# Work moved between VectorE, GpSimd and ScalarE where the attention heads give way to the sequence product

## The chip, the cores and the metric

One core of one Trainium2 chip runs the whole program. The metric is device time in microseconds of one execution; the time of the kernel before is the median of three runs. The engines are TensorE (PE in the profile, its weight loads PEld), VectorE (DVE), ScalarE (ACT), GpSimd (POOL) and SyncE (SP), which issues all the transfers that matter here. Each engine executes its own instructions in program order and waits for the others at semaphores.

## The reference

The network has four layers on one sequence of 2048 rows and 640 columns: attention, Fourier mixing, attention, Fourier mixing. Each adds its result to its input, and each normalizes its input first.

```python
def _A_ref(x, wqkv, wo):
    B, S, D = x.shape
    H = 32; Dh = D // H; W = 256
    qkv = (x @ wqkv).reshape(B, S, 3, H, Dh).transpose(2, 0, 3, 1, 4)
    q, k, v = qkv[0], qkv[1], qkv[2]
    scores = jnp.einsum("bhqd,bhkd->bhqk", q, k) * (Dh ** -0.5)
    scores = jnp.where(mask, scores, -1e9)  # 0 <= row - column < 256
    o = jnp.einsum("bhqk,bhkd->bhqd", _softmax(scores), v)
    return o.transpose(0, 2, 1, 3).reshape(B, S, D) @ wo

def _B_ref(x, dft_seq_re, dft_seq_im, dft_hid_re, dft_hid_im):
    a = jnp.einsum("bsd,ed->bse", x, dft_hid_re)
    b = jnp.einsum("bsd,ed->bse", x, dft_hid_im)
    return jnp.einsum("ts,bse->bte", dft_seq_re, a) - jnp.einsum("ts,bse->bte", dft_seq_im, b)

x = x + _A_ref(_layernorm(x), A_wqkv, A_wo)
x = x + _B_ref(_layernorm(x), ...)      # and both once more
```

## The kernel before

**Precision.** All large products are taken three times in a reduced float format: each operand is cut into a high half (ScalarE, L157) and a low half, the rest (a subtraction at L163, on VectorE or on the engine that the caller names). Product = high·high + high·low + low·high.

**The passage from heads to sequence product** is what the change touches; it occurs twice, once after each attention layer. At the end of the heads the output projection is done in two parts. The first three of its five input chunks are done while the heads still run (*partials*, L847); the last two ("late" chunks, k = 3 and 4) come afterwards, one 128-row tile t = 0 to 15 at a time (*late*, L925 to L964). The late operands are loaded per block of four tiles, one *late set* sb = 0 to 3 (*load_o*, L738): two chunks arrive by DMA (L751) with the reciprocal softmax sums (L757), are multiplied (L769, tile names cr, x, pt) and cut into halves in the tiles kp (L157, L163). These steps are not done at once but posted: *post(delay, fn)* puts fn into a slot, and *tick* runs what is due, so a posted instruction enters its engine's program order some slots later. After the heads a tick is counted for every 0.65 us of TensorE work (*spend*).

**A tile of late** is two products of 6 matmuls (L170) in the banks 5 and 6 alternately, each followed by an addition on VectorE (L940, or L934 for the first four tiles) that frees the bank. Then follow the statistics (L215, L217, L219, L946), the inverse root as a power on GpSimd (L948), two ScalarE steps that normalize (L904, L901), and the cuts of the normalized rows x (*split_x*, tile name big). Tiles 0 to 7 give the upper half of x, tiles 8 to 15 the lower; for the lower half the sum of two tiles is made (*sum1*, L1008) and a difference (*sum3*, L1012). The last two tiles take a shorter way, with VectorE normalizing their last 256 columns (*norm_last*, L916).

**The sequence product** multiplies the transposed DFT matrix, loaded in tiles of 128 x 1024 (L1103, DRAM tensor c), with x. Symmetries of the matrix and a seven-product scheme reduce the matmuls: for a (sb, part) of the output the order is a list of units (phase, j), and for the first (sb, part) it is: a1 for j = 0 to 7, a2 for j = 0 to 6, b7 0, a2 7, b7 1, b5 0, b5 1, b 2 to 7, g 0 to 7. a1 units need tile j of x, a2 units need tile j + 8, so these units are run between the tiles of late (*after_heads*, L972). The other three (sb, part) have phases a, b, g only.

A unit is run by *seq(n)* (L1191): it issues loads for a few units ahead, cuts the matrix of unit n + 1 (*cut_to*), prepares x for n + 1 (*x_to*), issues the matmuls (L1220) and cuts the matrix of unit n + 2. Cutting an a1 matrix first makes a difference t1 of its two halves (L1138), used later in a2; a b matrix has a difference on VectorE (L1146); a g matrix has two (L1149 t1, L1150 p) and three cuts. The b7 units have their difference at L1111 and two cuts. The sums of x for phase b are made pair by pair on VectorE (*sum4_to*, L1020 and L1021).

All eight PSUM banks are in use at the end of phase b. After the last unit of a phase *gather* (L1248) copies the sums out of the banks: for a1 three copies on ScalarE (L1269, L1270), for a2 one on ScalarE and one on VectorE (L1272, L1273), for b an addition, two ScalarE copies and two VectorE copies (L1264, L1280, L1283), which free banks for the first g unit. Its stores are kept in a list and issued one unit later or more.

What sets the order is the program text with its posted slots; there is no planner. The lines on which the steps rest:

```python
 768        eng, at = (nc.vector, (6, 8)) if self.after else (nc.gpsimd, (8, 10))
 948            self.post(2, lambda st=st: nc.gpsimd.tensor_tensor(
1138                nc.gpsimd.tensor_tensor(out=t1, in0=q, in1=p, op=OP.subtract)
1149                nc.gpsimd.tensor_tensor(out=t1, in0=p, in1=t1, op=OP.subtract)
1156                self.split(c[0], c[1], x, eng=nc.gpsimd if ph == "a2" and j > 5 else None)
1239        self.cut_to(n + 2)
1240        if last:
1241            self.gather(sb, part, ph)
```

Of the kernel before, what the change touches and what calls it, by code (L numbers as in the profile page):

```python
# [33 lines left out]
EARLY = 3  # L34
# [3 lines left out]
FIRST = 7  # L38
LATE = 9
PACE = 0.65  # L40


CHUNKS = ((0, 16, 0, 8), (0, 16, 8, 16), (16, 24, 0, 16), (24, 32, 0, 16), (0, 32, 16, 20))
# [18 lines left out]
class Net:  # L62
# [222 lines left out]
    def attention(self, xsrc, xdst):  # L285
        self.take_small(F32)
        for name in ("kp", "qp"):
            for i in (1, 0):
                if (name, i) != ("kp", 0):
                    self.take_qk(name, i)  # L290
        self.after, self.wide, self.lead = False, False, True
        self.late_o, self.late_t = [], 0
        self.before_heads(xsrc)
        self.heads(xsrc, xdst, self.fourier_hook)
        self.after_heads()
# [442 lines left out]
    def load_o(self, o, sb, k, raw=None, rr=None):  # L738

        nc = self.nc  # L740
        raw = self.raw()[:, :512] if raw is None else raw
        h0, h1, d0, d1 = CHUNKS[k]
        for q in range(h0 // 4, h1 // 4):
            while (q, sb) not in self.stored:
                if self.heavy:
                    self.relieve()
                self.tick()
        cols = slice(sb * 512, (sb + 1) * 512)
        nh, nd = h1 - h0, d1 - d0
        src = self.od[h0:h1, 1 + d0:1 + d1, cols]  # L750
        nc.sync.dma_start(raw, src if nh >= nd else src.rearrange("h d s -> d h s"))  # L751
        if k and CHUNKS[k - 1][:2] == (h0, h1):
            rr = self.turn.pop(("rr", sb))
        else:
            rr = self.next("rr") if rr is None else rr
            src = self.rd[sb, h0:h1, :]
            nc.sync.dma_start(rr, src.unsqueeze(1).broadcast_to([nh, nd, 512]) if nh >= nd else  # L757
                              src.unsqueeze(0).broadcast_to([nd, nh, 512]))
            self.turn["rr", sb] = rr
        o["left"] = o.get("left", 0) + 1  # L760

        def done():
            o["left"] -= 1

        def cut():
            self.split(o[k][0], o[k][1], raw, eng=nc.gpsimd)
            self.post(0 if k < EARLY else 3, done)
        eng, at = (nc.vector, (6, 8)) if self.after else (nc.gpsimd, (8, 10))
        self.post(at[0], lambda: eng.tensor_tensor(out=raw, in0=raw, in1=rr, op=OP.mult))  # L769
        self.post(at[1], cut)  # L770

    def complete(self, o):
        while o["left"]:
# [121 lines left out]
    def late(self, xsrc, xdst, hook):  # L895
# [29 lines left out]
        for t in range(NB):  # L925
# [9 lines left out]
            else:  # L935
# [8 lines left out]
            st = self.stats(xw, False)  # L944
            nm = self.ln.tile([P, 2], F32, name="nb", tag="nb")
            nc.vector.tensor_scalar_mul(nm[:, 0:1], st[0][:, 0:1], -1.0)  # L946
            fast = t >= NB - 2
            self.post(2, lambda st=st: nc.gpsimd.tensor_tensor(  # L948
                out=st[1][:, 1:2], in0=st[1][:, 0:1], in1=self.half, op=OP.pow))
            if NB // 2 - 1 <= t < NB - 1:  # L950
                self.post(4, lambda t=t: self.sum3(t - NB // 2 + 1))
            if fast:
# [19 lines left out]
    def after_heads(self):  # L972
# [4 lines left out]
        while True:  # L977
            t = self.late_t
            self.poll_late(99)
            while t < NB and not self.ready_late():  # L980
                if not self.unit():
                    self.tick()
                self.poll_late(99)
# [11 lines left out]
                self.tick()  # L995
        for _ in range(20):
            self.tick()
        assert not self.posted
        self.slot = None


# [118 lines left out]
    def cut_to(self, n):  # L1120
        nc = self.nc
        while self.n_cut <= min(n, len(self.order) - 1):
# [4 lines left out]
            ph, j = self.order[u][2:]  # L1127
            if ph == "b7":
                if j:
                    self.staged(u, 0, nc.gpsimd)  # L1130
                    self.staged(u, 1)
                    self.staged(u, 2)
                continue
            t1, r = self.t1[j], self.raw_of.pop(u, None)
            if r is not None:
                p, q = r[:, :512], r[:, 512:]
            if ph in ("a", "a1"):
                nc.gpsimd.tensor_tensor(out=t1, in0=q, in1=p, op=OP.subtract)  # L1138
                src = [p] + ([t1] if ph == "a" else [])
            elif ph == "a2":  # L1140
                src = [t1]
# [3 lines left out]
            elif ph == "b":  # L1145
                nc.vector.tensor_tensor(out=p, in0=q, in1=p, op=OP.subtract)  # L1146
                src = [q, p]
            else:
                nc.gpsimd.tensor_tensor(out=t1, in0=p, in1=t1, op=OP.subtract)  # L1149
                nc.vector.tensor_tensor(out=p, in0=t1, in1=q, op=OP.subtract)  # L1150
                src = [q, t1, p]
            out = []
            for x in src:
                c = self.ring.popleft()
                self.ring.append(c)
                self.split(c[0], c[1], x, eng=nc.gpsimd if ph == "a2" and j > 5 else None)
                out.append(c)
            self.cut_of[u] = out

    def x_to(self, n):  # L1160
# [30 lines left out]
    def seq(self, n):  # L1191
# [42 lines left out]
        if ph == "g":  # L1234
            mul("m1", x[0], 0, 256, c[0])
            mul("c1", x[0], 256, 128, c[0])
            mul("m6", x[1], 0, 256, c[1])
            mul("m4", x[0], 384, 256, c[2])
        self.cut_to(n + 2)
        if last:  # L1240
            self.gather(sb, part, ph)

    def leave(self, n=9):
# [4 lines left out]
    def gather(self, sb, part, ph):  # L1248
# [16 lines left out]

        mid = self.pt[2][:, 1024:]
        if ph in ("a", "a1"):
            for i in range(2):
                nc.scalar.activation(m1[i], banks("m1")[i], AF.Copy)  # L1269
            nc.scalar.activation(mid, banks("c1")[0], AF.Copy)  # L1270
        if ph in ("a", "a2"):
            nc.scalar.activation(m5[0], banks("m5")[0], AF.Copy)  # L1272
            nc.vector.tensor_copy(m5[1], banks("m5")[1])  # L1273
        if ph == "b":
            out = self.raw()[:, :512]
            add(nc.vector, out, banks("c2")[0], mid)
# [250 lines left out]
```

## Time and profile before

| | |
|---|---|
| median of 3 runs | 2259.83 us (2257.31 to 2260.46) |
| profiled execution, its own time | 2260.54 us |
| its span, first to last instruction | 2258.8 us |
| mean granted TensorE clock | 0.987 |
| first passage, late tiles and first (sb, part) up to g 0 | about 549 to 672 us of the span |
| second passage | about 1665 to 1788 us of the span |

A row of the view by stretches gives start and end in us from the span's start, the length, the busy time (and number of instructions) of TensorE, weight loads, VectorE, ScalarE and GpSimd, the granted clock as a fraction of full speed, the share of the DMA engines and GB/s. A row of the waits names who waited for whom: us in total, how often, the longest. A row of the groups gives line, engine, operation, tiles out<-in, shapes and count, then busy us and mean ns of one, then the idle time of the engine before it and what ended it. A row of the timeline has start, duration, engine, line and tiles, and in brackets the idle time before it with the engine that ended it. A row of the chain of work that ended last has start, duration and who held it.

### The profile page before, as it was taken

To read this page: it belongs to the slowest core of one execution; us is meant where nothing else is said; L and a number is where in the kernel's file an instruction comes from. 1 tells how busy PE (TensorE), PEld (TensorE's weight loads), DVE (VectorE), ACT (ScalarE), POOL (GpSimd) and SP (SyncE) were. 2 spreads that over 40 slices of the span, in tenths; PEclk is the share of its full clock that TensorE was granted. 3 is DMA by queue.
4 is the path that set the end of the run, shared out by engine and by line. 5 is a ranking of instruction groups with operands and counts; after the bars stand their busy time and mean duration, and the time that the engine had idled before them with its cause. 6 is when DMAs were issued, how large, how long until landed. Compare 5 with 4: busy or idle time off the path is not lost. (4 is left out here: it accounts for less than half of the span.)

```text
span 2258.8 us, 49233 instructions
## 1 busy us (share of the span) xinstructions
PE 2169.5 (96%) x18064; PEld 1817.8 (80%) x18064; DVE 1489.8 (66%) x3705; ACT 1114.2 (49%) x2401; POOL 1014.9 (45%) x1540
## 2 busy tenths in 40 slices
PE   7999999998889999999999999999998899999999
PEld 7987777677768888889999777777776688888999
DVE  6347788674787868772461578876746968678522
ACT  2117777656454545541331277776655545446310
POOL 3037776767745223230130477678676433232200
PEclk9999999899999999999999999998999999999999
DMA  5545656775435353655446465668753354545553
GB/s 180 179 143 186 195 185 198 220 208 163 138 117 182 125 183 131 214 170 168 161 165 190 142 194 179 202 195 233 198 170 120 117 183 139 168 156 201 164 166 100
DMA packets 217297, 385.57 MB, mean 171 GB/s; under 512 B 38880, under 2 KB 85472, under 8 KB 217056
## 3 DMA queue, kind: packets, MB, share of 16 engines
q1 hardware_dynamic: 217056, 382.43, 53.2%
q8 instruction: 143, 2.34, 0.5%
q14 instruction: 98, 0.80, 0.1%
HBM read 267.39 MB, written 113.77 MB: 169 GB/s over the span
## 5 line engine op out<-in xcount | busy, mean ns | idle before, releaser
L553 DVE CUSTOM_DVE_ANT_0 banks<-banks,mask 128x384 f32<-128x384 f32 (+2 forms) x1024 | 526.7, 557 | 174.7 <-PE banks L548 125.7
L582 ACT ACTIVATE pt<-banks 128x384 f32<-128x384 f32 (+2 forms) x1024 | 430.8, 469 | 209.4 <-PE banks L548 115.0
L573 PE MATMUL banks<-qp,kp 61*128 61x384 f32 (+2 forms) x1024 | 320.0, 376 | 10.7 <-ACT pt L582 9.2
L588 POOL TENSOR_SCALAR_AFFINE_SELECT pt<-pt 128x256 f32<-128x256 f32 x512 | 208.1, 407 | 206.9 <-ACT pt L582 156.5
L548 PE MATMUL banks<-kp,qp 60*128 60x384 f32 (+2 forms) x1024 | 285.5, 367 | 11.4 <-DVE mc L553 10.7
L188 PE MATMUL banks<-big,wc 64*128 64x512 f32 x1920 | 266.9, 392 | 0.4 <-DVE pt L371 0.4
L573 PEld LDWEIGHTS banks<-qp,kp 61*128 61x128 f32 x1024 | 178.8, 187 | 78.6 <-ACT pt L582 43.9
L603 PE MATMUL banks<-pt,vq 128*32 128x128 f32 x5760 | 220.3, 281 | 8.8 <-POOL pt L588 8.8
L188 PEld LDWEIGHTS banks<-big,wc 64*128 64x128 f32 x1920 | 186.4, 186 | 20.1 <-DVE pt L371 0.5
L163 DVE TENSOR_TENSOR qp<-pt,qp 128x512 fp32r<-128x512 f32 (+1 forms) x209 | 167.7, 811 | 50.8 <-ACT qp L157 50.0
L603 PEld LDWEIGHTS banks<-pt,vq 128*32 128x32 f32 x5760 | 146.1, 111 | 67.1 <-issue 52.2
L548 PEld LDWEIGHTS banks<-kp,qp 60*128 60x128 f32 x1024 | 164.8, 188 | 32.9 <-DVE mc L553 23.6
L592 POOL TENSOR_SCALAR_AFFINE_SELECT pt<-pt 128x256 f32<-128x256 f32 x448 | 182.7, 408 | 0.0
L157 ACT ACTIVATE qp<-pt 128x512 fp32r<-128x512 f32 (+1 forms) x209 | 128.9, 624 | 104.6 <-DMA pt<-c 36.5
L1220 PE MATMUL banks<-qp,big 128*128 128x512 f32 x630 | 153.4, 394 | 6.1 <-POOL big L163 4.3
L1149 POOL TENSOR_TENSOR pt<-pt,pt 128x512 f32<-128x512 f32 x40 | 59.7, 1496 | 203.7 <-DMA pt<-c 134.8
L1408 DVE TENSOR_TENSOR x<-banks,x 128x320 f32<-128x320 f32 x64 | 29.8, 488 | 178.6 <-DMA x<-x_d 108.8
L553 DVE DVE_READ_ACCUMULATOR2_ANT mc<- 128x1 f32 x1024 | 144.9, 141 | 0.0
L1220 PEld LDWEIGHTS banks<-qp,big 128*128 128x128 f32 x630 | 118.2, 189 | 32.0 <-POOL big L163 5.8
L157 ACT ACTIVATE c<-pt 128x512 fp32r<-128x512 f32 x144 | 88.2, 624 | 74.9 <-DVE pt L1146 36.0
L163 DVE TENSOR_TENSOR c<-pt,c 128x512 fp32r<-128x512 f32 x140 | 112.3, 814 | 14.9 <-ACT c L157 12.6
L170 PE MATMUL banks<-big,pt 128*128 128x320 f32 x768 | 118.2, 309 | 0.9 <-DVE pt L1345 0.9
(201 smaller groups left out, 4430.5 us busy)
## 6 DMA issues: line engine op xcount, KB each, us to landing
pt<-c SPq DMA_DIRECT2D x188, 512.0 KB
qk_d<-c SPq DMA_DIRECT2D x80, 512.0 KB
kp<-qk_d SPq DMA_DIRECT2D x384, 80.0 KB
qp<-qk_d SPq DMA_DIRECT2D x384, 80.0 KB
kp<-u_d SPq DMA_DIRECT2D x32, 640.0 KB
o_d<-ou SPq DMA_DIRECT2D x64, 256.0 KB
x_d<-x SPq DMA_DIRECT2D x48, 320.0 KB
v_d<-pt SPq DMA_DIRECT2D x16, 768.0 KB
```

Of the source, the lines that this page charges most:

```text
L157: nc.scalar.activation(hi, src, AF.Copy, scale=-1.0 if neg else 1.0)
L163: (eng or nc.vector).tensor_tensor(out=lo, in0=src, in1=hi.bitcast(F32), op=OP.subtract)
L170: self.nc.tensor.matmul(p, x, y, start=n == 0, stop=n == last)
L188: self.nc.tensor.matmul(ps[a], x[r], y[r], start=half + i == 0, stop=half == 1 and i == n - 1, skip_group_check=True)
L548: nc.tensor.matmul(p, qp[quad % 2][b:b + 60, z, qb * P:(qb + 1) * P], kp[quad % 2][b:b + 60, z, k0 * P:(qb + 1) * P], start=True, stop=True)
L553: nc.vector.tensor_tensor_reduce(out=p, in0=p, in1=self.mask[:, 384 - n * P:], scale=1.0, scalar=NEG, op0=OP.add, op1=OP.max, accum_out=mc ...
L573: nc.tensor.matmul(self.banks[:, e, :n * P], kp[quad % 2][b:b + 61, z, kb * P:(kb + 1) * P], qp[quad % 2][b:b + 61, z, kb * P:(kb + n) * P ...
L582: nc.scalar.activation(pt[quad, kb][:, 2 * z + e0:2 * z + e1, :n * P], self.banks[:, e0:e1, :n * P], AF.Exp, scale=SCALE)
L588: nc.gpsimd.affine_select(out=t[:, :, 0:P], in_=t[:, :, 0:P], pattern=[[0, 2], [1, P]], compare_op=OP.is_ge, fill=0.0, base=0, channel_mul ...
L592: nc.gpsimd.affine_select(out=t[:, :, 256:384], in_=t[:, :, 256:384], pattern=[[0, 2], [-1, P]], compare_op=OP.is_gt, fill=0.0, base=0, ch ...
L603: nc.tensor.matmul(p[32 * h:32 * h + 32, :], vq[:, 96 * (kb % 4) + 21 * h:96 * (kb % 4) + 21 * h + 32], t[:, h, (qb - kb) * P:(qb - kb + 1 ...
L1220: nc.tensor.matmul(self.banks[:, bk, :], p, b[q], start=start and m == 0, stop=stop and last and m == 2, skip_group_check=True)
```

## The change

It touches only the passage. Part by part:

- *Late sets*: multiplication and low halves of the late chunks (k of 3 and 4) are on VectorE always; before, the multiplication was on GpSimd while the heads still ran and the low half always on GpSimd.
- *Scaling behind the next additions*: after the heads, the multiplication is not issued at its slot but put into a list, *held*, which *let_go* empties behind the statistics of the next late tile, or while a set is waited for. The cut follows two slots later.
- *Root of the last two tiles* (t of 14 and 15): issued at once instead of two slots later.
- *First matrix differences*: in the first (sb, part) the difference t1 of the a1 units is on VectorE; so is t1 of g 0 and g 1, and there q is cut first, then t1 is made and cut, then p.
- *b7 1*: its difference is on VectorE instead of GpSimd, and the sums of x for j = 0 to 3 are issued there.
- *a2 6 and a2 7*: the low half of the matrix is on VectorE instead of GpSimd.
- *Gather of the first phase b* is issued ahead of the cut of g 1 instead of behind it.
- *Copies spread*: the three ScalarE copies of the a1 gather are posted 1, 4 and 7 slots later; of the a2 gather's two copies the VectorE one goes to ScalarE.

```diff
@@ load_o @@
+        eng = nc.gpsimd if k < EARLY else nc.vector
+
         def cut():
-            self.split(o[k][0], o[k][1], raw, eng=nc.gpsimd)
+            self.split(o[k][0], o[k][1], raw, eng=eng)
             self.post(0 if k < EARLY else 3, done)
-        eng, at = (nc.vector, (6, 8)) if self.after else (nc.gpsimd, (8, 10))
-        self.post(at[0], lambda: eng.tensor_tensor(out=raw, in0=raw, in1=rr, op=OP.mult))
-        self.post(at[1], cut)
+
+        def scale():
+            eng.tensor_tensor(out=raw, in0=raw, in1=rr, op=OP.mult)
+            self.post(2, cut)
+        if self.after:
+            self.post(6, lambda: self.held.append(scale))
+        else:
+            self.post(8, scale)
+
+    def let_go(self):
+        while self.held:
+            self.held.pop(0)()
@@ late @@
             nc.vector.tensor_scalar_mul(nm[:, 0:1], st[0][:, 0:1], -1.0)
+            self.let_go()
             fast = t >= NB - 2
-            self.post(2, lambda st=st: nc.gpsimd.tensor_tensor(
-                out=st[1][:, 1:2], in0=st[1][:, 0:1], in1=self.half, op=OP.pow))
+
+            def root(st=st):
+                nc.gpsimd.tensor_tensor(out=st[1][:, 1:2], in0=st[1][:, 0:1], in1=self.half, op=OP.pow)
+            if fast:
+                root()
+            else:
+                self.post(2, root)
@@ after_heads @@
             while t < NB and not self.ready_late():
+                self.let_go()
                 if not self.unit():
                     self.tick()
@@ cut_to @@
             if ph == "b7":
                 if j:
-                    self.staged(u, 0, nc.gpsimd)
+                    self.staged(u, 0, nc.vector)
                     self.staged(u, 1)
                     self.staged(u, 2)
+                    self.sum4_to(SOON)
                 continue
...
+            first = self.order[u][:2] == (0, 0)
+            out = []
+
+            def cut(x):
+                c = self.ring.popleft()
+                self.ring.append(c)
+                self.split(c[0], c[1], x)
+                out.append(c)
             if ph in ("a", "a1"):
-                nc.gpsimd.tensor_tensor(out=t1, in0=q, in1=p, op=OP.subtract)
+                (nc.vector if first else nc.gpsimd).tensor_tensor(out=t1, in0=q, in1=p, op=OP.subtract)
                 src = [p] + ([t1] if ph == "a" else [])
...
+            elif first and j < 2:
+                cut(q)
+                nc.vector.tensor_tensor(out=t1, in0=p, in1=t1, op=OP.subtract)
+                cut(t1)
+                nc.vector.tensor_tensor(out=p, in0=t1, in1=q, op=OP.subtract)
+                src = [p]
             else:
                 nc.gpsimd.tensor_tensor(out=t1, in0=p, in1=t1, op=OP.subtract)
                 nc.vector.tensor_tensor(out=p, in0=t1, in1=q, op=OP.subtract)
                 src = [q, t1, p]
-            out = []
             for x in src:
-                c = self.ring.popleft()
-                self.ring.append(c)
-                self.split(c[0], c[1], x, eng=nc.gpsimd if ph == "a2" and j > 5 else None)
-                out.append(c)
+                cut(x)
@@ seq @@
+        soon = last and ph == "b" and not sb + part
+        if soon:
+            self.gather(sb, part, ph)
         self.cut_to(n + 2)
-        if last:
+        if last and not soon:
             self.gather(sb, part, ph)
@@ gather @@
         if ph in ("a", "a1"):
-            for i in range(2):
-                nc.scalar.activation(m1[i], banks("m1")[i], AF.Copy)
-            nc.scalar.activation(mid, banks("c1")[0], AF.Copy)
+            for i, (out, src) in enumerate(zip(m1 + [mid], banks("m1") + banks("c1"))):
+                self.post(1 + 3 * i, lambda out=out, src=src: nc.scalar.activation(out, src, AF.Copy))
         if ph in ("a", "a2"):
             nc.scalar.activation(m5[0], banks("m5")[0], AF.Copy)
-            nc.vector.tensor_copy(m5[1], banks("m5")[1])
+            if ph == "a":
+                nc.vector.tensor_copy(m5[1], banks("m5")[1])
+            else:
+                nc.scalar.activation(m5[1], banks("m5")[1], AF.Copy)
```

SOON is 4. The list *held* is made empty in *attention*.

More of the change, by code (lines that the diff above doesn't have):

```diff
@@ L291, in attention @@
         self.after, self.wide, self.lead = False, False, True
-        self.late_o, self.late_t = [], 0
+        self.late_o, self.late_t, self.held = [], 0, []
         self.before_heads(xsrc)
@@ L997, in after_heads @@
             self.tick()
-        assert not self.posted
+        assert not self.posted and not self.held
         self.slot = None
```

1 line of the change is left out of this document (added).

## The prediction

> **What bounds the kernel now.** The first view is the page's share of busy time, the second the granted clock and the idle time by stretch of the two places that the change touches, the third what TensorE waited for there.
>
> ```profile
> PE 2169.5 (96%) x18064; PEld 1817.8 (80%) x18064; DVE 1489.8 (66%) x3705; ACT 1114.2 (49%) x2401; POOL 1014.9 (45%) x1540
> ```
> ```profile
> 553.40:571.00 17.60, 13.38 (x52) 10.22 (x50) 9.76 (x23) 7.39 (x15) 16.77 (x15) 0.81 0.81 254
> 571.00:597.00 26.00, 23.72 (x128) 20.53 (x126) 18.66 (x49) 13.07 (x25) 21.29 (x21) 1.00 0.57 181
> 597.00:613.00 16.00, 13.30 (x74) 11.58 (x74) 11.08 (x30) 9.47 (x20) 10.72 (x16) 1.00 0.27 105
> 613.00:626.50 13.50, 10.79 (x40) 7.97 (x40) 8.78 (x21) 7.26 (x16) 8.12 (x10) 0.87 0.34 120
> 626.50:659.30 32.80, 30.12 (x122) 21.75 (x121) 28.75 (x45) 15.72 (x39) 14.43 (x17) 1.00 0.33 112
> 659.30:672.00 12.70, 8.68 (x30) 6.34 (x29) 12.39 (x15) 7.03 (x13) 5.99 (x5) 0.87 0.34 105
> 1669.40:1687.00 17.60, 13.23 (x52) 10.11 (x50) 9.77 (x23) 7.44 (x15) 16.77 (x15) 0.81 0.83 253
> ```
>
> Columns are length, busy time of TensorE, its weight loads, VectorE, ScalarE and GpSimd, then granted clock. TensorE is the kernel's bound nearly everywhere, but in the passage from heads to sequence product it idles 18.6 us of 118.6 (the first six rows) and runs below full clock in three of six stretches. The second attention layer repeats the first (last row against the first), so I work out one layer and double it.
>
> ```profile
> PE banks L170 <- DVE x L940: 5.0, 4, 1.9
> PE banks L1220 <- DVE c L163: 3.4, 1, 3.4
> PE banks L1220 <- DVE rr L163: 2.4, 6, 0.5
> PE banks L1220 <- POOL big L163: 2.1, 2, 1.2
> PE banks L1220 <- ACT c L157: 1.9, 1, 1.9
> PE banks L170 <- POOL kp L163: 1.1, 1, 1.1
> ```
> ```profile
> 1676.82 1.68 POOL pt L1138
> 1678.50 2.46 POOL kp L163 x2
> 1706.28 3.00 POOL kp L163 x2
> ```
>
> The waits name VectorE most, but the chain of work that ended last shows who is really late: in the second layer's copy of the first stretch it is a GpSimd queue of matrix differences (L1138) and late-set halves (kp, L163), the instructions that the change moves. GpSimd is busy 16.77 of 17.60 us there, VectorE 9.76.
>
> **First stretch, 553.4 to 597 (43.6 us).** What moves from GpSimd to VectorE:
>
> ```profile
> L1138 POOL TENSOR_TENSOR pt<-pt 128x512 f32<-128x512 f32 x3 | 4.8, 1588 | 0.0
> L163 POOL TENSOR_TENSOR kp<-pt,kp 128x512 fp32r<-128x512 f32 x3 | 3.9, 1301 | 3.0 <-ACT kp L157 3.0
> L1138 POOL TENSOR_TENSOR ou<-pt 128x512 f32<-128x512 f32 x2 | 2.6, 1300 | 0.0
> L769 POOL TENSOR_TENSOR cr<-cr,rr 128x512 f32<-128x512 f32 x2 | 2.5, 1296 | 0.0
> L163 POOL TENSOR_TENSOR kp<-cr,kp 128x512 fp32r<-128x512 f32 x2 | 2.5, 1264 | 0.0
> L163 POOL TENSOR_TENSOR kp<-x,kp 128x512 fp32r<-128x512 f32 x1 | 1.8, 1758 | 0.0
> L1138 POOL TENSOR_TENSOR pt<-s 128x512 f32<-128x512 f32 x1 | 1.3, 1282 | 0.0
> L1138 POOL TENSOR_TENSOR vq<-pt 128x512 f32<-128x512 f32 x1 | 1.3, 1275 | 0.0
> ```
> ```profile
> L163 DVE TENSOR_TENSOR qp<-pt,qp 128x512 fp32r<-128x512 f32 x6 | 5.7, 942 | 4.3 <-ACT qp L157 4.3
> L769 DVE TENSOR_TENSOR pt<-pt,vq 128x512 f32<-128x512 f32 x1 | 1.8, 1770 | 0.0
> L163 DVE TENSOR_TENSOR qp<-s,qp 128x512 fp32r<-128x512 f32 x1 | 1.8, 1764 | 0.6 <-ACT qp L157 0.6
> L769 DVE TENSOR_TENSOR pt<-pt,rr 128x512 f32<-128x512 f32 x2 | 1.3, 678 | 0.0
> ```
>
> GpSimd loses 20.7 us (the sum of the first block) and keeps 38.06 - 20.7 = 17.4: it is no bound any more. VectorE gets 15 instructions. The undisturbed price of one is 0.68 us (L769, 678 ns). VectorE's busy time of 28.4 becomes 28.4 + 15 x 0.68 = 38.6. Collisions with GpSimd now cost 3.8 of that (6 x 0.26 in the first L163 row, and 1.1 each in the two rows near 1.77); with GpSimd half empty I take half of them away: 36.7. VectorE keeps its order, so it can't be filled whole. In the stretches where it is the bound today it is filled to 0.88 (28.75 of 32.80) and 0.976 (12.39 of 12.70); between, at 0.93, it needs 39.4 us. TensorE would need 13.38 x 0.81 + 23.72 = 34.6 at full clock, so VectorE is the new bound, and the low clock of the first row goes as far as the idle time does. **Gain 4.2 us**; ends: 36.7 / 0.976 = 37.6 (gain 6.0) and 38.6 / 0.88 = 43.9 (loss 0.3).
>
> This takes in the held scaling. Today TensorE stands still in front of an addition that is queued behind it:
>
> ```profile
> 589.10 2.03 PE L170 MATMUL banks<-qp,kp 128*128 128x320 f32 x12 [1.93 <-DVE x L940]
> ```
>
> The 1.77 L769 above is that obstacle; held until the statistics behind the next addition are issued, it runs where TensorE already has its banks back. The wait that this adds is on set 2 and 3 becoming ready about one tile later; the loop in after_heads issues ticks or matrix units meanwhile, so TensorE has work, and I put nothing on it (a tile's 2 us if that cover is gone, inside the range). In the heads, set 0 leaves GpSimd too, but TensorE has no gap there: nothing. No DMA moves past another; the early gather only files its stores, and they leave as before.
>
> **597 to 613.** Two of the four L940 waits (1.88 and 0.81; the row's 5.0 is these, 1.93 and 0.35) lie here, 2.7 idle. Both follow GpSimd's last two kp halves (the 3.00 us chain row), through the normalization and ScalarE's casts to the L163 in front of L940. The halves go; the three copies of the a1 sums, back to back on ScalarE today, are spread. VectorE is busy 11.08 of 16.0 and gets nothing here. **Gain 2.0** (0 to 2.7): the second, short wait may stay.
>
> **613 to 626.5.** The root of the last two tiles is issued at once instead of two ticks later.
>
> ```profile
> 616.12 0.54 POOL L948 TENSOR_TENSOR rs<-rs,half 128x1 f32<-128x1 f32 x1
> 616.70 0.82 DVE L916 TENSOR_SCALAR big<-x,mv,rs 128x256 f32<-128x256 f32 x1 [1.14 <-POOL rs L948]
> ```
>
> VectorE's 1.14 us wait for it goes, and with it most of TensorE's wait in the ACT c row. The low halves of the last two a2 sets go to VectorE, 0.68 for about 1.3 each, but behind the statistics of the last tile, which gives the shorter duration back. **Gain 1.3** (0 to 2.9: the 2.7 of idle and a little clock).
>
> **626.5 to 672 (45.5 us).** VectorE is the bound: 41.1 busy. Here come and go: the b7 difference (+0.68), two t1 of the g sets (+1.36), the m5 copy that goes to ScalarE (-0.69). The sums of x only move, into an early hole:
>
> ```profile
> L1020 DVE TENSOR_TENSOR big<-big 128x256 f32<-128x256 f32 x8 | 6.0, 747 | 0.0
> ```
> ```profile
> 625.71 1.85 POOL L1111 TENSOR_TENSOR pt<-pt 128x512 f32<-128x512 f32 x1
> 627.59 0.63 ACT L157 ACTIVATE qp<-pt 128x512 fp32r<-128x512 f32 x1 [1.91 <-POOL pt L1111]
> ```
> ```profile
> 658.11 4.36 POOL L1149 TENSOR_TENSOR pt<-pt,pt 128x512 f32<-128x512 f32 x3
> 659.61 1.73 DVE L1150 TENSOR_TENSOR pt<-pt,pt 128x512 f32<-128x512 f32 x1 [1.18 <-POOL pt L1149]
> 663.08 3.65 PE L1220 MATMUL banks<-c,xc 128*128 128x512 f32 x8 [3.37 <-DVE c L163]
> ```
>
> With the difference on VectorE the 1.9 us behind GpSimd goes, and the sums fill it; four sums are two instructions each, 8 x 0.75 = 6.0 at the mean of their row and less with GpSimd idle; what the hole doesn't hold stands ahead of the piece of x that the next b7 unit needs, some 1 to 2 us for TensorE, given back because later steps have fewer sums. In the g sets the 1.18 wait and the stretching of L1150 (1.73 against 0.68) go, and TensorE's 3.37 wait with them, for q is cut first. What is late next: TensorE needs the banks that the gather's L1264 frees, queued behind g 0's three cuts, and the second g set comes after that. New holes: VectorE waits for ScalarE's high half twice in each of the two sets, 4 x 0.63 = 2.5. So 41.1 + 1.35 - 1.05 (L1150) - about 1.0 (other collisions) = 40.4 busy; holes 4.4 - 1.9 - 1.2 + 2.5 = 3.8; 0.9 of the new ones I take as covered by casts that are ready early: 43.3. **Gain 2.2** (0 to 5.1, the latter if VectorE were full).
>
> **Sum.** 4.2 + 2.0 + 1.3 + 2.2 = 9.7 a layer, 19.4 for two. The profiled execution took 2260.5 us (span 2258.8, 1.7 around it) and becomes 2241.1; it lies 0.7 above the median, so 2240.
>
> **Rivals.** *VectorE not the bound.* All of TensorE's idle and slow time of the first three stretches goes: 9.0 + 2.7 + 4.1 (13.5 less 10.79 x 0.87), and the fourth as forecast: 18.0 a layer, 2224. For it: GpSimd held the chain. Against: 36.7 of VectorE's work is more than TensorE's 34.6. Chance 0.12.
>
> *The normalization stays as slow.* Its root and its halves remain on GpSimd, and a VectorE instruction on two SBUF tiles stops them:
>
> ```profile
> 575.45 0.87 DVE L163 TENSOR_TENSOR qp<-pt,qp 128x512 fp32r<-128x512 f32 x1
> 575.73 1.00 POOL L948 TENSOR_TENSOR rs<-rs,half 128x1 f32<-128x1 f32 x1
> ```
>
> Against the undisturbed root (0.54 above) a collision costs 0.46; one for each of eight tiles takes 3.7 off the first gain. 6.0 a layer remain: 2248. Chance 0.22. The Trainium skill ("SBUF — State Buffer", section "Who interferes with whom") has the same as a rule: a VectorE instruction with two SBUF inputs and a GpSimd one that reads SBUF lock each other out, the later one fully. The trace agrees (1.00 against 0.54); by the rule the moved work would lock GpSimd out 15 times, and the sum would go toward this rival.
>
> *Slower: the addition L940 is late behind the moved work.* VectorE is in order, so each moved instruction can stand ahead of the L940 that frees TensorE's two banks. If they cost the mean of undisturbed and collided, (0.68 + 1.77) / 2 = 1.22, VectorE needs 28.4 + 15 x 1.22 = 46.7, and 47.9 at 0.976 filled: 4.3 lost a layer, with nothing won later since the next stretches start late: 2268. It decides from (43.6 x 0.93 - 28.4) / 15 = 0.81 us apiece. Against: GpSimd has 20.7 us less to collide with. Chance 0.10.
>
> *Nothing changes*: what one stretch wins the g sets hand back through their four new holes and the bank wait; 2260. Chance 0.06.
>
> **Numbers.** The forecast (2232 to 2247 with its bounds) has 0.50. Faster by over 0.2%, about what this kernel's measurement can tell from no change, means below 2255.3: 0.50 + 0.12 + 0.22 = 0.84; same 0.06; slower 0.10. The range leaves out the slower case and the far end of the first rival: 2226 to 2257.
>
> **What would show it.** First stretch: GpSimd near 17 us, VectorE 36 to 39, clock near 1.0, shorter by 4; no L163 kp in the waits of TensorE. The 1.93 wait before L170 gone. Copies L1269 apart, L940 waits below 1 us in the second. L916 waiting under 0.3 us. The 3.37 wait gone, in its place waits for L1264 and for the second xc. It is wrong if VectorE's moved instructions average over 0.81 us, if L940 stays the longest wait, or if the stretch to 672 ends no earlier than VectorE's old 45.5.

## The result and the profile after

| | before | after |
|---|---|---|
| median | 2260.14 us (2255.43 to 2263.13, 6 runs) | 2246.53 us (2244.74 to 2251.64, 6 runs) |
| ratio | | 0.9942 [0.9925, 0.9959] |
| profiled execution, span | 2260.5, 2258.8 | 2245.7, 2243.8 |

The change made the kernel 13.6 us faster; the forecast was about 20. The time lies in the range, but the passage did not do what the steps said. In the page's share of busy time, work has gone from GpSimd to VectorE and little else is seen:

```profile
PE 2156.4 (96%) x18064; PEld 1815.4 (81%) x18064; DVE 1518.4 (68%) x3753; ACT 1115.3 (50%) x2403; POOL 957.0 (43%) x1490
```

To compare kernels I set time zero at the first a1 matmul of a passage and ask when certain units start. The four stretches below run from a1 0 to a2 1, on to b7 1, to g 0 and to g 3, each taken where that unit starts (columns as in the prediction: length, TensorE, weight loads, VectorE, ScalarE, GpSimd, clock). First the kernel before, then after:

```profile
553.35:600.80 47.45, 39.06 (x192) 32.71 (x191) 31.28 (x79) 22.91 (x44) 40.13 (x40) 0.93 0.66 211
600.80:628.60 27.80, 24.27 (x109) 19.30 (x109) 17.39 (x44) 15.30 (x32) 17.83 (x22) 0.94 0.25 89
628.60:659.30 30.70, 28.02 (x112) 20.09 (x112) 28.41 (x45) 14.71 (x37) 13.37 (x16) 1.00 0.35 120
659.30:679.70 20.40, 16.38 (x64) 12.73 (x63) 20.09 (x28) 11.72 (x22) 8.39 (x6) 0.92 0.36 116
```
```profile
547.65:592.60 44.95, 38.13 (x190) 31.94 (x190) 42.09 (x96) 25.18 (x48) 26.64 (x29) 0.96 0.70 223
592.60:615.30 22.70, 22.22 (x110) 18.51 (x109) 19.14 (x46) 13.79 (x29) 11.70 (x16) 1.00 0.32 106
615.30:646.00 30.70, 26.96 (x113) 21.75 (x112) 27.87 (x45) 14.81 (x37) 11.69 (x16) 0.94 0.36 120
646.00:670.20 24.20, 17.74 (x65) 13.57 (x64) 19.62 (x28) 11.51 (x22) 9.44 (x5) 0.86 0.30 99
```

Row by row: the first is 2.5 us shorter, with VectorE now filled to 42.09 of 44.95. The second is 5.1 shorter and TensorE all but full. The third is as long as it was. The fourth is 3.8 longer, although VectorE works less in it: its idle time rose from 0.3 to 4.6 us, and the clock fell from 0.92 to 0.86. The longest of TensorE's waits in this passage (who <- for whom: us in total, times, longest):

```profile
PE banks L1250 <- DVE rr L164: 3.7, 1, 3.7
PE banks L1250 <- ACT xc L158: 3.6, 1, 3.6
PE banks L171 <- DVE x L952: 3.0, 2, 2.5
PE banks L1250 <- DVE x L1297: 2.9, 1, 2.9
PE banks L1250 <- DVE qp L164: 1.7, 1, 1.7
PE banks L171 <- DVE kp L164: 1.0, 1, 1.0
```

GpSimd's kp halves and the long waits for c are gone from the list; in their place stand one wait for rr, the low half of a piece of x that b7 1 needs, and two waits in the g sets (xc and L1297). L952 is the addition that was L940.

A wait here can cost more than its length, because the granted clock is low behind it. After the wait for rr, seven matmuls took 3.0 us at a clock of 0.50, and the next thirteen 2.6 us at 1.00:

```profile
619.70:622.70 3.00, 3.00 (x7) 2.42 (x8) 2.91 (x5) 1.44 (x4) 1.25 (x2) 0.50 0.11 19
622.80:625.40 2.60, 2.60 (x13) 2.17 (x12) 1.08 (x2) 1.07 (x3) 0.13 (x1) 1.00 0.47 180
```

It does not follow each wait. Here is the wait for L952 in the first and in the second passage. It is equally long, but the twelve matmuls behind it took 3.37 us in the one and 2.02 in the other:

```profile
585.58 3.37 PE L171 MATMUL banks<-qp,kp 128*128 128x320 f32 x12 [2.54 <-DVE x L952]
1696.33 2.02 PE L171 MATMUL banks<-qp,kp 128*128 128x320 f32 x12 [2.53 <-DVE x L952]
```

All kernels of the study in one table. Start of three units after the first a1 matmul, first and second passage, from the profiled execution; then the median of the undisturbed runs, and its ratio to the runs of the kernel before that were taken with it:

```
kernel        b7 1          g 0            g 3              median (runs)   ratio to before [interval]
before        75.28 75.10   105.98 105.98  126.38 126.36    2260.14 (6)
after         67.65 67.32    98.32  99.08  122.52 122.14    2246.53 (6)     0.9942 [0.9925, 0.9959]
late_only     71.27 71.28   102.14 102.14  122.54 122.56    2252.50 (10)    0.9968 [0.9957, 0.9979]
a1_back       69.36 69.76   100.24  99.27  123.42 121.88    2249.54 (6)     0.9951 [0.9929, 0.9973]
no_sums       67.79 67.32    97.00  96.55  120.51 119.64    2241.05 (4)     0.9921 [0.9904, 0.9939]
old_g         67.25 67.77    99.22  98.67  121.23 120.87    2245.93 (4)     0.9944 [0.9926, 0.9963]
before_again  75.58 75.27   106.40 105.45  128.44 125.88    2259.14 (1)
after_again   67.85 67.83    98.70  98.68  121.65 121.75    2246.73 (4)     0.9934 [0.9912, 0.9956]
held_off      67.55 67.54    99.59  99.19  122.67 122.13    2246.04 (4)     0.9935 [0.9920, 0.9950]
g_order       67.56 67.31    96.79  96.56  116.42 115.85    2234.95 (4)     0.9893 [0.9870, 0.9916]
g_xb          67.53 68.04    95.24  95.75  115.45 114.34    2235.30 (4)     0.9889 [0.9867, 0.9911]
g_a1pool      69.39 69.37    98.62  98.60  119.83 117.90    2240.57 (4)     0.9918 [0.9898, 0.9937]
hold_cut      68.90 68.80    96.72  96.75  116.02 116.08    2237.29 (4)     0.9911 [0.9888, 0.9933]
```

So the change had won 7.6 to 7.8 us per passage by b7 1, kept 6.9 to 7.7 to g 0, and held 3.9 to 4.2 at g 3.

### The profile page after: what moved, and what is told of

Read it like the earlier page. It is cut to its first block, busy times and chain, and to the rows that moved or that the text cites. A ratio compares the mean times of both kernels' runs of the same rounds, so it can differ in the third digit from the quotient of the medians.

```text
span 2243.8 us, 49235 instructions
## 1 busy us (share of the span) xinstructions
PE 2156.4 (96%) x18064; PEld 1815.4 (81%) x18064; DVE 1518.4 (68%) x3753; ACT 1115.3 (50%) x2403; POOL 957.0 (43%) x1490
## 4 chain that ended last, share of the span: by engine, by line
PE 40%; DVE 4%; POOL 2%; ACT 2%; issue 1%; DMA 1%; SPq 0%; ACTq 0%; DVEq 0%; POOLq 0%
PE banks L1250 14%; PE banks L171 12%; PE banks L189 6%; PE banks L604 3%; PE banks L574 3%; PE banks L549 2%; ACT pt L583 1%; POOL c L475 0%; DMA vq<-v_d 0%; POOL pt L589 0%; POOL ou L1183 0%; DVE banks L554 0%; DVE c L164 0%; PE banks L271 0%; ACT qp L158 0%
## 5 line engine op out<-in xcount | busy, mean ns | idle before, releaser
L549 PE MATMUL banks<-kp,qp 60*128 60x384 f32 (+2 forms) x1024 | 280.9, 362 | 8.4 <-DVE mc L554 7.4
L1250 PE MATMUL banks<-qp,xc 128*128 128x512 f32 x480 | 121.7, 400 | 5.9 <-ACT xc L158 5.7
```

The source lines that it names most:

```text
L549: nc.tensor.matmul(p, qp[quad % 2][b:b + 60, z, qb * P:(qb + 1) * P], kp[quad % 2][b:b + 60, z, k0 * P:(qb + 1) * P], start=True, stop=True)
L1250: nc.tensor.matmul(self.banks[:, bk, :], p, b[q], start=start and m == 0, stop=stop and last and m == 2, skip_group_check=True)
```

## The experiments

**late_only: the late sets alone.** The kernel before, with only the two late chunks' multiplication and low halves on VectorE, not held.

```diff
-            self.split(o[k][0], o[k][1], raw, eng=nc.gpsimd)
+            self.split(o[k][0], o[k][1], raw, eng=nc.gpsimd if k < EARLY else nc.vector)
-        eng, at = (nc.vector, (6, 8)) if self.after else (nc.gpsimd, (8, 10))
+        eng, at = (nc.gpsimd if k < EARLY else nc.vector, (6, 8) if self.after else (8, 10))
```

> The kernel before with one part of the change: multiplication and low halves of the late sets on VectorE, at the slots they had. Measure: the time from the first a1 matmul to the first matmul of g 3 in each layer's passage (before 126.4 and 126.4 us, after 122.5 and 122.1). Theory 1 (GpSimd's queue was late, and freeing it is the gain; what VectorE takes on is paid back only where VectorE then has no room): GpSimd loses 10.7 us before a2 0, VectorE gets 5.4, and a2 0 comes 2 to 4 us earlier than 41.4; the passage is 123 to 124.5. Rival (the late sets were hidden, the a1 differences were the queue): a2 0 within 1 us of 41.4 and the passage 125.5 or more. The time outside the passages: if its 7 us of difference between the two profiles belong to the change's text, this run has the first a1 matmul near 553 as before; if they are variation from execution to execution, it may lie anywhere between 547 and 554.

Each passage was 3.8 us shorter at g 3, nearly as much as with the whole change. It did not come about as expected: a2 0 started at 42.67 and 41.12 us, not 2 to 4 earlier than 41.4, and the gain arose between a2 0 and b7 1. There it stands at 4.0 and 3.8, and nothing gives it back, for the rest of the order is the old one. So within the passages this one part carries what the change keeps, and the other parts together won a further 3.6 to 4.0 up to b7 1 and lost it behind. The medians say less: this kernel is 6.9 us faster than the one before and still 6.0 slower than the one after, and the passages account for little of those 6.0.

**a1_back: the a1 differences on GpSimd again**, all else as after.

```diff
-                (nc.vector if first else nc.gpsimd).tensor_tensor(out=t1, in0=q, in1=p, op=OP.subtract)
+                nc.gpsimd.tensor_tensor(out=t1, in0=q, in1=p, op=OP.subtract)
```

> The changed kernel with the a1 differences of the first (sb, part) back on GpSimd. Theory 1a (VectorE is the new bound up to a2 0, busy 42.2 of 45.3 us there while GpSimd is busy 27.0): taking eight instructions of 0.68 to 1.5 us off VectorE makes a2 0 come 1 to 3 us earlier than 41.1, the passage 120 to 122.5. Rival (GpSimd's queue is what counts): GpSimd gets 10 us back, split and root come late again, a2 0 at 42 or later, the passage 123.5 or more.

The a1 4 unit starts 2.4 and 1.9 us later than in after, b7 1 1.7 and 2.4 later, but g 3 only 0.9 later in the one passage and 0.3 earlier in the other; the median is 3.0 higher, and the intervals overlap. Neither expectation came: a2 0 was 0.4 us later in both passages, where theory 1a had it earlier and the rival had it at 42 or later. What the move wins up to b7 1 is lost again in the stretch with the wait for rr (b5 0: 0.8 and 0.9 left) and behind it.

**no_sums: the early sums of x left to their old place.**

```diff
-                    self.sum4_to(SOON)
```

> The changed kernel without the early sums of x at b7 1; each sum is made where it was before. Theory 2 (the eight sum instructions stand in front of the piece of x that b7 1 needs, cost 3.7 us there and save the same later, since VectorE is the bound from b7 to g either way): the 3.7 us wait of b7 1 falls under 1 us, the b units take 4.05 us apiece again instead of 3.4, and g 0 comes within 1 us of 98.3 after the first a1 matmul. Rival (the early sums are what makes the b units faster, a true gain): g 0 at 100.5 or later, the passage 124 or more.

g 3 is 2.0 and 2.5 us earlier and the median 5.5 us lower. That refutes the rival, and it is more than theory 2 said, by which the early sums only moved time: g 0 came 1.3 and 2.5 us earlier too. The timeline of VectorE and TensorE in after (start, duration, engine, line, tiles, in brackets the wait) shows why:

```profile
614.66 0.96 DVE L1039 TENSOR_TENSOR big<-big 128x256 f32<-128x256 f32 x1
...
618.98 0.42 DVE L1040 TENSOR_TENSOR kp<-big,big 128x256 f32<-128x256 f32 x1
619.32 0.28 DVE L164 TENSOR_TENSOR rr<-big,rr 128x128 fp32r<-128x128 f32 x1
```
```profile
619.66 0.80 PE L1250 MATMUL banks<-qp,rr 128*128 128x512 f32 x1 [3.74 <-DVE rr L164]
```

Eight sum instructions fill 614.66 to 619.32 without a pause, and the small rr that TensorE needs stands behind them. There was no hole for them to fill: with the b7 difference on VectorE, the wait that made the hole was gone.

**old_g: the g sets and the gather in the old order**, all else as after.

```diff
-            elif first and j < 2:
+            elif first and j < 0:
-        soon = last and ph == "b" and not sb + part
+        soon = False
```

> The changed kernel with g 0 and g 1 cut as before (difference t1 on GpSimd, then p, then three cuts) and the gather of phase b behind the cut of g 1 again. Theory 3 (the new order of the g sets gives back 2.9 to 3.8 us: VectorE waits about 0.7 us for ScalarE five times, and the gather's L1297 and the second xc come late): g 0 to g 2 takes 15.6 as before or less, against 19.4, and the passage is 119 to 121. Rival (the give-back is VectorE's backlog, which any order has): g 0 to g 2 takes 18 or more, and the passage is 122 or more.

g 3 comes 1.3 us earlier than in after, though g 0 is within 0.9 either way: from g 0 to g 2 it took 17.25 and 17.44 us, after took 19.44 and 18.30, before 15.64. That lies between theory 3 (15.6 or less) and its rival (18 or more). So the new order costs something as it is written. That the old one is slower here than in before says little: the unchanged kernel before took 17.28 us in one of the four passages that were profiled. What decides between 15.6 and 17.3 was not followed up. In after VectorE stands idle in it again and again, for ScalarE:

```profile
646.97 1.01 DVE L164 TENSOR_TENSOR c<-pt,c 128x512 fp32r<-128x512 f32 x1 [0.70 <-ACT c L158]
...
649.61 0.69 DVE L164 TENSOR_TENSOR qp<-pt,qp 128x512 fp32r<-128x512 f32 x1 [1.03 <-ACT qp L158]
650.22 0.68 DVE L1297 TENSOR_TENSOR x<-banks,pt 128x512 f32<-128x512 f32 x1
...
654.00 1.72 DVE L164 TENSOR_TENSOR qp<-pt,qp 128x512 fp32r<-128x512 f32 x1 [0.70 <-ACT qp L158]
...
657.02 0.69 DVE L164 TENSOR_TENSOR rr<-pt,rr 128x512 fp32r<-128x512 f32 x1 [0.70 <-ACT rr L158]
```
```profile
651.05 1.62 PE L1250 MATMUL banks<-c,vq 128*128 128x512 f32 x6 [2.85 <-DVE x L1297]
657.66 4.29 PE L1250 MATMUL banks<-qp,xc 128*128 128x512 f32 x9 [3.61 <-ACT xc L158]
```

Each low half is asked for right behind the difference that it is the rest of, so ScalarE has had no time to make the high half. The addition L1297, which frees a bank, stands behind two of these waits, the second set behind two more.

**before_again and after_again: both kernels unchanged**, for the spread of the parts that nobody touched.

> The kernel before, unchanged, for a second profile. Theory 4 (the difference of the two first profiles outside the passages, 1.7 us at the start, 4.1 in the first heads and 1.4 in the second, is variation from execution to execution): the passages take 126.4 us again to 0.1, while the first a1 matmuls lie elsewhere than at 553.4 and 1669.3 by 1 to 5 us. Rival (these belong to the kernel's text): first a1 matmul at 553 to 554 and at 1669 to 1670.

> The changed kernel, unchanged, for a second profile beside the experiments. Theory 4: passages 122.5 and 122.1 again to 0.3, the first a1 matmul within 5 us of 547.7 but not at it, and the median within 3 us of 2246.5.

Passages of the kernel before came out at 128.44 and 125.88, not at 126.4 to 0.1; those of after were 121.65 and 121.75. Span less both passages was 2006.1 and 2003.0 us for before and 1999.1 and 2005.1 for after; over all kernels here it ranged from 1998.7 to 2006.8 with no tie to an edit. The mean passage went from 126.8 to 122.0, 9.5 us for two. So both expectations for the passages failed, and a single passage of one kernel can differ by 2.6 us. The other 4 of the 13.6 us lie outside the passages, and what makes them was not found. They do not lie behind the passages: from g 3 to g 0 of the last (sb, part) it is 279.48 us in all thirteen profiles, both times, although the change spreads the copies of the a gathers there too. What varies lies ahead of each passage, in the heads: the first a1 matmul comes at 544.9 to 553.4 us. The code there is not quite the same, for the change also alters the order in which GpSimd takes the multiplications and low halves of the early chunks (the third multiplication of a set starts 2.7 us behind the second, not 5.2); no run tries that alone.

**held_off: the scaling at its slot instead of held.**

```diff
-            self.post(6, lambda: self.held.append(scale))
+            self.post(6, scale)
```

> The changed kernel with the scaling of the late sets posted at its slot instead of held behind the statistics of the next tile; all else as changed. Theory 5 (holding moves the multiplication, but the two low halves that follow two slots later stand in front of the next addition again, so holding saves nothing): the longest wait of the late products for an addition stays 1.9 to 3.0 us and a2 0 comes within 0.6 us of 41.1 (39.8 in the second layer). Rival (holding works, and its gain of some 2 us is hidden by VectorE's load): that wait is 3.5 us or more and a2 0 comes 1 us later or more.

TensorE's waits for L952 were four of 0.98, 0.60, 0.62 and 0.82 us, while after, with the holding, has one of 2.5 and a short one; g 3 differed by 0.15 and 0.01. So holding wins nothing, as theory 5 had it, but its two measures failed: the longest wait is shorter without the holding, and a2 0 comes 1.7 and 0.4 us earlier, all of which is lost again by b7 1. The timeline of VectorE in after shows how the holding itself makes the one long wait:

```profile
580.58 1.05 DVE L773 TENSOR_TENSOR pt<-pt,vq 128x512 f32<-128x512 f32 x1
581.55 0.68 DVE L773 TENSOR_TENSOR x<-x,vq 128x512 f32<-128x512 f32 x1
582.16 1.23 DVE L164 TENSOR_TENSOR c<-pt,c 128x512 fp32r<-128x512 f32 x1
583.31 0.68 DVE L164 TENSOR_TENSOR kp<-pt,kp 128x512 fp32r<-128x512 f32 x1
583.91 1.21 DVE L164 TENSOR_TENSOR kp<-x,kp 128x512 fp32r<-128x512 f32 x1
585.04 0.88 DVE L952 TENSOR_TENSOR x<-banks,big 128x320 f32<-128x320 f32 x2
```

Both scalings are let go in one place behind the statistics, and their low halves two slots later: 4.5 us of moved work in a row in front of the next addition at 585.04.

**hold_cut: the low halves held too**, on g_order (below).

```diff
-            self.post(2, cut)
+            if self.after and k >= EARLY:
+                self.held.append(cut)
+            else:
+                self.post(2, cut)
...
-        while self.held:
-            self.held.pop(0)()
+        now, self.held = self.held, []
+        for f in now:
+            f()
```

> This kernel is g_order in which the low half of a late weight piece waits behind the next addition too, not its scaling alone. Theory that the held scaling gains nothing because the low halves (0.68 and 1.21 in a row at 583.31) still stand in front of the next addition: the longest wait of a TensorE matmul of the last heads on an addition (L952) falls from 2.5 to below 1.2, the a2 0 to a2 6 stretch is 0.5 to 1.5 us shorter, g 3 as much earlier. Rival, that the lows then arrive late for the b units or only move in time on a full VectorE: g 3 within 0.3 of g_order or later.

The longest wait for that addition (L956 in this kernel) fell to 0.8 and a2 0 came 2.9 and 1.6 us earlier than in g_order. But at b7 1 the kernel was 1.3 and 1.5 us behind it, and at g 3 the two differ by -0.4 and +0.2. Three of TensorE's waits show the exchange; that for c was 0.5 in g_order, and that for big (L917) was not there:

```profile
PE banks L1252 <- DVE c L164: 1.8, 1, 1.8
PE banks L171 <- DVE x L956: 1.4, 3, 0.8
PE banks L171 <- ACT big L917: 1.4, 1, 1.4
```

The wait that was removed on a full VectorE came back later in the same passage. That is the rival, within 0.1 us.

**g_order: no early sums, and g sets whose low halves do not wait for ScalarE.** The gather stays early.

```diff
-                    self.sum4_to(SOON)
...
-                cut(q)
                 nc.vector.tensor_tensor(out=t1, in0=p, in1=t1, op=OP.subtract)
-                cut(t1)
+                cut(q)
                 nc.vector.tensor_tensor(out=p, in0=t1, in1=q, op=OP.subtract)
-                src = [p]
+                src = [t1, p]
```

> The changed kernel without the early sums, and with g 0 and g 1 still differenced on VectorE but in the order t1, cut of q, p, cut of t1, cut of p, so that VectorE has an instruction to do while ScalarE makes a high half. Theory 3a (the waits for ScalarE are what the new g order costs): g 0 to g 2 takes 15.5 to 17 instead of 18.8 (18.3) without the sums, the passage 117 to 118.7, and the time about 2237. Rival (VectorE's backlog alone): g 0 to g 2 at 18 or more, the passage 119.6 or more.

g 3 is 4.1 and 3.8 us earlier than in no_sums and 6.1 and 6.3 earlier than in after, and the ratio to before is 0.9893 [0.9870, 0.9916]: faster than both kernels. The same four stretches as above:

```profile
547.07:592.00 44.93, 38.16 (x191) 31.93 (x191) 42.02 (x96) 25.28 (x48) 26.64 (x29) 0.96 0.70 224
592.00:614.60 22.60, 22.14 (x109) 18.45 (x108) 19.11 (x46) 13.69 (x29) 11.57 (x16) 1.00 0.31 106
614.60:643.80 29.20, 27.17 (x112) 20.19 (x111) 27.78 (x45) 15.04 (x38) 11.49 (x16) 1.00 0.36 127
643.80:663.50 19.70, 16.83 (x65) 12.65 (x65) 17.99 (x27) 11.11 (x21) 9.40 (x4) 0.91 0.37 121
```

From g 0 to g 3 it takes 19.7 us against 24.2 in after and 20.4 in before. The order alone makes most of that: no_sums, from which this kernel differs by the order only, took 23.5. No instruction was taken away there; between each difference and the cut of its result now stands the cut of something else. VectorE's idle time in the stretch is 1.7 us instead of 4.6. Theory 3a's 15.5 to 17 us from g 0 to g 2 were bettered (14.86 and 14.54).

**g_xb: g_order with the low halves of the sums on VectorE instead of GpSimd.**

```diff
-            self.parts(self.xb[j], self.s3[j], 256, self.nc.gpsimd)
+            self.parts(self.xb[j], self.s3[j], 256)
-            self.parts(self.xb[j], self.s4[j], 0, self.nc.gpsimd)
+            self.parts(self.xb[j], self.s4[j], 0)
```

> This kernel is g_order with one thing moved: the eight low halves of the sums (the kp<-s and kp<-kp subtractions, 0.74 each on GpSimd beside VectorE's rr and halving) run on VectorE. Theory that the two engines slow each other there (rr 0.82 against 0.28 alone, the halving 0.95 against 0.41): rr and the halving fall back to below 0.50 each, the 0.37 to 0.54 waits per b unit shrink to below 0.2, and b5 0 to g 0 is 1 to 3 us per layer shorter than 27.2, time 2229 to 2234. Rival, that VectorE is the bound there too and only gets more work: b5 0 to g 0 at 27.2 or above, time 2235 to 2241.

A low half in the b units of g_order on GpSimd, and VectorE's instructions that run at the same time as such a one:

```profile
624.08 0.74 POOL L164 TENSOR_TENSOR qp<-s,qp 128x256 fp32r<-128x256 f32 x1 [2.59 <-ACT qp L158]
```
```profile
624.14 0.83 DVE L164 TENSOR_TENSOR rr<-big,rr 128x128 fp32r<-128x128 f32 x1
620.82 0.95 DVE L1039 TENSOR_TENSOR big<-big 128x256 f32<-128x256 f32 x1
```

and in g_xb, where GpSimd is silent:

```profile
624.16 0.28 DVE L164 TENSOR_TENSOR rr<-big,rr 128x128 fp32r<-128x128 f32 x1
624.36 0.42 DVE L164 TENSOR_TENSOR qp<-s,qp 128x256 fp32r<-128x256 f32 x1
...
625.03 0.42 DVE L1039 TENSOR_TENSOR big<-big 128x256 f32<-128x256 f32 x1
```

A unit's two new ones, 0.42 each, cost less than the collisions did (0.55 on rr and 0.53 on the halving). From b5 0 to g 0 VectorE now has 55 instructions:

```profile
620.15:645.85 25.70, 25.02 (x104) 18.50 (x103) 24.43 (x55) 14.31 (x35) 0.00 (x0) 1.00 0.37 127
```

against these in g_order:

```profile
616.60:643.80 27.20, 25.17 (x104) 18.55 (x103) 25.85 (x40) 13.71 (x35) 10.97 (x15) 1.00 0.34 120
```

With 15 more, VectorE is busy 1.4 us less, and the stretch is 25.67 us in both passages where it was 27.17 and 27.21: 1.5 less, as the theory had it. TensorE's five waits for VectorE's rr, 2.0 us in all in g_order, are gone; one of 0.7 for ScalarE's rr is new. The Trainium skill ("SBUF — State Buffer", "Who interferes with whom") says that a VectorE instruction with two inputs in SBUF and a GpSimd one that reads SBUF shut each other out; the pair 0.83 and 0.28 agrees. The median did not follow (2235.30 against 2234.95, where 2229 to 2234 was expected): a gain of 3 us is inside the spread of four runs, so a gain in time is not shown.

**g_a1pool: g_order with the a1 differences on GpSimd again** (the edit of a1_back).

> This kernel is g_order with the first a1 unit's eight differences on GpSimd again. Theory that the move of the differences gives nothing once VectorE also carries the late sets: a1 4 is 1 to 2.4 us later than in g_order and g 3 within 0.7 of 116.42/115.85. The prediction's step, that the move removes a wait that nothing gives back: g 3 is 2 us or more later in each layer, time at least 4 us above g_order.

a1 4 is 2.4 us later and g 3 3.4 and 2.1 us later; the median is 5.6 higher. That is the prediction's step, and not the theory. In the kernel of after the same edit left 0.9 and -0.3. So the move of the differences is worth 5.5 us where the waits behind it are gone; in after, most of it is lost behind b7 1.

## Why the prediction was partly right

**What bounds the passage: right.** VectorE did become the bound, filled to 42.09 of 44.95 in the first stretch (0.936; 0.93 was forecast). The clock there rose from 0.93 to 0.96 in the first passage and to 1.00 in the second; near 1.0 was forecast.

**VectorE's load: too low.** The fifteen moved instructions were priced at 0.68 us. Up to the end of a2 0 they took 13.0 us, 0.87 each, and VectorE was busy 41.2 us instead of 36.7, for it also executed nine instructions more, of later tiles. GpSimd was busy 25.0 us, not 17. The prediction gave 0.81 apiece as a sign of being wrong, and that sign came. Two of the dearer groups, with the mean ns of one:

```profile
L1166 DVE TENSOR_TENSOR pt<-pt 128x512 f32<-128x512 f32 x3 | 2.9, 955 | 0.0
L164 DVE TENSOR_TENSOR kp<-cr,kp 128x512 fp32r<-128x512 f32 x2 | 2.1, 1082 | 0.0
```

**The first three stretches: the sum right, its terms not.** The prediction's stretches end where a2 0 ends and about where a2 4 and a2 7 start. For them 4.2, 2.0 and 1.3 were forecast. The first gave 0.3 us in the first passage and 1.6 in the second, the next 3.3 in both, the third 4.0 and 2.0. At b7 1 the gain was 7.6 and 7.8, and 7.5 was forecast; with terms as far off as these, the agreement is partly luck.

**Held scaling: wrong.** At a1 7 the passage was 4.5 us ahead. In front of a2 0 most of that was lost, to the L952 wait of 2.5 us (L940's was 1.93) and, in the first passage, to the low clock behind it. "It runs where TensorE already has its banks back" failed: the step followed the scaling and forgot that its low half comes two slots later. Without the holding (held_off) the longest such wait is 0.98.

**Root of the last tiles: right in its mechanism.** VectorE's L928, the old L916, no longer waits for the root:

```profile
602.35 1.00 POOL L963 TENSOR_TENSOR rs<-rs,half 128x1 f32<-128x1 f32 x1
```
```profile
603.47 0.83 DVE L928 TENSOR_SCALAR big<-x,mv,rs 128x256 f32<-128x256 f32 x1
```

**626.5 to 672: the term that failed.** Forecast +2.2, measured from b7 1 to g 3 -3.8 and -3.6 a passage. Up to the start of g 1, near the end of its stretch, 0.8 and 0.7 us were lost; the rest was lost behind it, where the step put nothing. It was put together from two sizes. The sums were to cost TensorE "some 1 to 2 us", given back later; the wait was 3.74, with a low clock behind it, and 2.0 to 2.5 us were never given back (no_sums). The sums were to fill a hole that the same change removes. The g sets' new holes were 2.5 with 0.9 covered; VectorE's idle time from g 0 to g 3 rose by 4.3. Both places were named, the wait at b7 1 and the waits for L1297 and the second xc, but no lasting gap of TensorE was put on them, and nothing on the clock: the step counted VectorE's work and holes, not what stood behind each hole in its order. That the stretch ends no earlier than before was another sign of being wrong that the prediction gave.

**Rivals.** The mechanism of "nothing changes", that the g sets hand back through their holes and the bank wait what was won before, did happen, with half of its price. That VectorE is not the bound is excluded by its 0.936. The slower case did not come, although its price of 0.81 was passed: the waits for the addition fell from 5.0 to 3.0 us in all. "The normalization stays as slow" has the time nearest to the measured one, 2248, and part of what it says is seen: up to the end of a2 0 the roots on GpSimd took 0.95 us each where they had taken 0.78, and the 128x384 halves of x 1.21 instead of 1.08. But it takes 3.7 us off the first gain for good, and by b7 1 the whole 7.5 were there; what was lost was lost behind it. TensorE's waits for a GpSimd half of x (POOL big) fell from 2.1 to 1.0. The normalization was not tried by itself, so its price stays open.

**The total.** 9.7 a layer was forecast, 4.8 is the mean of two executions. The time came nearer to the forecast than the passage did, by about 4 us that lie outside the passages, where nothing was forecast. They are not explained, so that the time lies in the range is partly luck.

## What to carry to other kernels

When work moves onto an engine that then becomes the bound, list its program order behind every move, and for each instruction that another engine waits for, what stands in front of it: here 0.28 us of work on which TensorE waited stood behind 4.7 us that nobody needed yet. Put a difference, then the cut of something else, then the cut of the difference, so that the engine that makes the high half runs beside it. Judge a part with the later waits removed: by the passages the same edit was worth 0.6 us in one order and 5.5 in another (3.0 and 5.6 by the medians). Count for a wait of TensorE not only its length, but look at the granted clock behind it.

## What was not expected of the hardware

Moving fifteen small subtractions onto the busiest engine of a stretch shortened it by 1.5 us in both passages, because the instructions there no longer collide: 0.28 us had been stretched to 0.83 and 0.42 to 0.95. The same wait of 2.5 us was followed by a low clock in one passage and not in the other, and a2 0 came 1.35 us later for it. And the part of the span outside the passages took from 1998.7 to 2006.8 us in single executions, all of the difference ahead of the passages, so a change of 4 us can be judged by the trace of its own place, but not by one execution's time.
